# A fixed order for the first layernorm tiles, the third tile's statistics on ScalarE, and three x tiles loaded ahead of w_in

## The chip, the cores and the metric

One core of one Trainium2 chip. The metric is the device time of one execution in microseconds (us), lower is better. The engines are called as the profile calls them: PE (TensorE matmuls), PEld (TensorE weight loads), DVE (VectorE), ACT (ScalarE), POOL (GpSimd), and SPq for the queue that issues the DMAs. A ratio is the mean time of one kernel's fast runs over the mean of the other's fast runs of the same rounds, so it is not quite the ratio of the medians quoted beside it.

## The reference, cut to what matters

```python
x = A_x                                     # 1 x 2048 x 640, bf16
xn = _layernorm(x, axis=-1)                 # every path starts here
return x + A(xn, ...) + B(xn, ...)
# B: z = gelu(xn @ w_in); z1, z2 = halves of z; z2 = layernorm(z2)
#    g = w_sp @ z2 + b_sp ("spatial");  result (z1 * g) @ w_out
# A: a state-space scan: Bu = xn @ B_bar, h[t] = L*h[t-1] + Bu[t], y = 2*Re(h @ C)
```

The 2048 rows are 16 tiles of 128 rows, x0 to x15. Nothing but warm-up can run on PE before tile 0 is loaded, normalised and transposed.

## The kernel before

Each step of the program is an operation with declared reads, writes and an estimated duration. A small scheduler in the program walks the operations in estimated time and fixes, for each engine, **one order of instructions**. Estimated times decide that order and nothing else. On the chip, each engine keeps its order and waits at the head of its queue, as DVE does below for 1.24 us.

```python
FIRST = "x0 x1 h002 x2 h025 x3 h105 x4 x5"     # order of the first loads on SPq
# x2: tile 2 (160 KB).  h002, h025: w_in's second half, columns 0-431, k tiles 0-1 and 2-4
# (216 and 324 KB).  h105: columns 432-863, k tiles 0-4 (540 KB)
...
NW = 11                                         # warm-up matmuls, 128x512, on a zero tile
...
ACT_LN = (6, 8, 10, 12)                         # tiles whose statistics ACT computes

def ln_x(i):
    if i in ACT_LN:
        act(Copy,   accum_out=sum)              # lnsum: two passes on ACT
        act(Square, accum_out=sum of squares)   # lnsq
        dve(mean); dve(mean*mean); dve(variance)          # lnm, lnmm, lnv: 128x1 each
    else:
        dve(bn_stats, x[:, 0:320]); dve(bn_stats, x[:, 320:640]); dve(bn_aggr)   # statistics a, b, aggregate
    dve(variance + 1e-5)                        # lne
    pool((variance + eps) ** -0.5)              # rstd
    dve((x - mean) * rstd)                      # xn, 128x640
# ... cut ...
for i in range(5):
    ln_x(i)
xn_T(0, 0)          # T0: five PE transposes, then copies of PSUM by ACT (3/5) and DVE (2/5)
xn_T(1, 1)          # T1
z2_half(0, 0, 2)    # ten 128x432 matmuls on tiles 0 and 1, w_in columns 0-431
z2_half(1, 0, 3)
xn_T(2, 0)          # T2
z2_half(0, 1, 6)
xn_T(3, 1)          # T3
# ... cut: from tile 6 on, the transposes are DMAs; then "bu" (B matmuls), z1, spatial, output
```

## Time and profile before

| | before |
|---|---|
| median of the first 3 runs | 267.07 us (267.0 to 268.37) |
| span of the profiled execution | 265.7 us |
| PE busy | 259.6 us (98%) |
| PE idle at the two first transposes | 1.27 + 0.45 us |
| PE idle at 21 us, for a DMA transpose | 0.35 us |

The page's first part gives busy time, share of the span and instruction count of each engine.

```profile
PE 259.6 (98%) x1517; PEld 154.3 (58%) x1521; DVE 239.1 (90%) x574; ACT 174.1 (66%) x315; POOL 24.5 (9%) x41
```

PE is the engine to feed, and its gaps are few. The next lines are the timeline of PE in the kernel before: start, duration, engine, source line, operation, tiles, count, and in brackets how long the engine had been idle and what ended it.

```profile
1.31 4.75 PE L485 MATMUL ps<-arena 128*128 128x512 bf16 x11 [1.31 <-POOL arena L479]
7.33 0.45 PE L558 MATMUL ps<-arena 128*128 128x128 bf16 x5 [1.27 <-DVE arena L542]
8.23 0.45 PE L558 MATMUL ps<-arena 128*128 128x128 bf16 x5 [0.45 <-DVE arena L542]
8.53 2.03 PE L615 MATMUL ps<-arena 128*128 128x432 bf16 x10
10.39 0.44 PE L558 MATMUL ps<-arena 128*128 128x128 bf16 x5
...
21.36 18.42 PE L594 MATMUL ps<-arena 128*128 128x432 bf16 x100 [0.35 <-DMA arena<-arena]
39.84 20.45 PE L677 MATMUL ps<-arena 128*128 128x512 bf16 x93
```

The lines are the warm-ups, T0, T1, the first z2 matmuls, T2, the wait for the first DMA-transposed tile, and the first "bu" matmuls. The next view is the same kernel's DVE timeline around the gap.

```profile
4.92 0.21 DVE L533 BATCH_NORM_AGGREGATE arena<-arena 128x2 f32<-128x12 f32 x1
6.37 0.50 DVE L531 BATCH_NORM_STATS2 arena<-arena 128x6 f32<-128x320 bf16 x1 [1.24 <-DMA arena<-in_A_x_dram]
6.78 0.14 DVE L535 TENSOR_SCALAR arena<-arena 128x1 f32<-128x1 f32 x1
6.84 0.44 DVE L542 TENSOR_SCALAR arena<-arena 128x640 bf16<-128x640 bf16 x1
```

At 5.13 DVE has finished tile 1's statistics. The next instruction in its queue is tile **2's** first statistics, and x2 has not landed. Behind it stand tile 1's epsilon add (6.78) and tile 0's normalise (6.84). Both could have run. T0 follows at 7.33.

### The profile page before, as it was taken

The numbers are of one execution on the slowest core, as the hardware profiler recorded it, in microseconds if no ns is written. First come the engines' busy times: TensorE is split into PE (matmuls) and PEld (weight loads), VectorE is DVE, ScalarE is ACT, GpSimd is POOL, SyncE is SP. The second block draws the span as 40 slices with busy tenths as digits, with TensorE's granted clock in tenths as the row PEclk, the third lists the DMA queues.
The fourth block names the chain that finished last, engine by engine and source line by source line (L and its number), as shares of the span: only waits on it lengthen the run. The fifth ranks groups of instructions, "written<-read, shape, count | busy, mean of one in ns | idle before, by whom it ended". The sixth has DMA issues, their size and how long they took to land.

```text
span 265.7 us, 4351 instructions
## 1 busy us (share of the span) xinstructions
PE 259.6 (98%) x1517; PEld 154.3 (58%) x1521; DVE 239.1 (90%) x574; ACT 174.1 (66%) x315; POOL 24.5 (9%) x41
## 2 busy tenths in 40 slices
PE   7899999999999999999999999999999999999996
PEld 2454554444446777755555545555567777777774
DVE  3899999998999999999999999999999999976342
ACT  2699999989997545533233294584999999931110
POOL 3345176104000000000000000000000000000000
DMA  6957799996002755499979978969343566755411
GB/s 173 366 77 125 165 222 233 294 228 127 0 0 45 210 164 163 116 263 136 218 157 202 225 139 191 218 147 276 86 135 92 128 180 147 182 147 125 120 52 49
DMA packets 88243, 41.98 MB, mean 158 GB/s; under 512 B 70974, under 2 KB 88222, under 8 KB 88222
## 3 DMA queue, kind: packets, MB, share of 16 engines
q1 hardware_dynamic: 88078, 41.66, 66.2%
q8 instruction: 12, 0.20, 0.3%
q14 instruction: 9, 0.07, 0.1%
q10 hardware_dynamic: 144, 0.05, 0.1%
HBM read 12.27 MB, written 12.45 MB: 93 GB/s over the span
## 4 chain that ended last, share of the span: by engine, by line
PE 63%; DVE 21%; DMA 5%; ACT 5%; issue 3%; POOL 1%; SPq 0%; DVEq 0%
PE ps L594 18%; PE ps L677 16%; PE ps L1111 14%; PE ps L1123 11%; DVE arena L949 4%; PE ps L992 4%; ACT arena L784 4%; DVE arena L1012 3%; DVE arena L729 3%; DMA arena<-arena 2%; DMA arena<-in_A_x_dram 2%; DMA arena<-in_B_w_sp_dram 2%; DVE arena L914 1%; DVE arena L1033 1%; DVE arena L707 1%
## 5 line engine op out<-in xcount | busy, mean ns | idle before, releaser
L992 PE MATMUL ps<-arena 128*128 128x432 bf16 x448 | 82.4, 346 | 0.0
L992 PEld LDWEIGHTS ps<-arena 128*128 128x128 bf16 x448 | 43.6, 98 | 38.7 <-ACT arena L1005 1.5
L594 PE MATMUL ps<-arena 128*128 128x432 bf16 x280 | 51.8, 346 | 0.3 <-DMA arena<-arena 0.3
L784 ACT ACTIVATE arena<-arena 128x512 bf16<-128x512 bf16 x70 | 45.3, 717 | 2.2 <-DVE arena L749 2.1
L594 PEld LDWEIGHTS ps<-arena 128*128 128x128 bf16 x280 | 34.6, 124 | 16.7 <-DMA arena<-arena 0.8
L1111 PE MATMUL ps<-arena 128*128 128x320 bf16 x280 | 43.3, 299 | 0.2 <-ACT ps L1146 0.2
L677 PE MATMUL ps<-arena 128*128 128x512 bf16 x196 | 43.0, 379 | 0.2
L1005 ACT ACTIVATE arena<-ps,arena 128x432 f32<-128x432 f32 (+1 forms) x32 | 19.6, 617 | 30.3 <-PE ps L992 30.2
L1123 PE MATMUL ps<-arena 128*128 128x320 bf16 (+3 forms) x231 | 35.6, 295 | 0.0
L1111 PEld LDWEIGHTS ps<-arena 128*128 128x128 bf16 x280 | 27.2, 97 | 11.4 <-ACT ps L1146 0.5
L677 PEld LDWEIGHTS ps<-arena 128*128 128x128 bf16 x200 | 19.6, 98 | 23.5
L1138 DVE TENSOR_TENSOR arena<-ps,arena 128x320 bf16<-128x320 f32 (+1 forms) x40 | 18.9, 487 | 11.9 <-PE ps L1123 11.3
L1123 PEld LDWEIGHTS ps<-arena 128*128 128x128 bf16 (+1 forms) x231 | 22.3, 98 | 8.3
L707 DVE SCALAR_TENSOR_TENSOR arena<-arena 128x512 f32<-128x512 bf16 x35 | 25.8, 748 | 0.4 <-ACT arena L683 0.4
L788 DVE TENSOR_TENSOR arena<-arena 128x1024 bf16<-128x1024 bf16 (+1 forms) x42 | 23.9, 599 | 0.1
L683 ACT CAST arena<-ps 128x512 bf16<-128x512 f32 x40 | 21.3, 606 | 2.7 <-PE ps L677 2.7
L663 ACT ACTIVATE arena<-ps 128x864 bf16<-128x864 f32 x16 | 14.3, 891 | 13.5 <-PE ps L594 13.4
L949 DVE TENSOR_TENSOR arena<-arena 128x1024 bf16<-128x1024 bf16 x32 | 21.1, 688 | 0.9 <-DMA arena<-in_B_w_sp_dram 0.9
L729 DVE TENSOR_TENSOR arena<-arena 128x512 f32<-128x512 f32 (+2 forms) x40 | 21.3, 554 | 0.0
L1146 ACT COPY ps<-ps 128x320 f32<-128x320 f32 x16 | 6.7, 417 | 15.9 <-PE ps L1111 15.9
L709 DVE SCALAR_TENSOR_TENSOR arena<-arena 128x256 bf16<-128x256 bf16 (+1 forms) x35 | 16.7, 479 | 0.0
L712 DVE SCALAR_TENSOR_TENSOR arena<-arena 128x256 bf16<-128x256 bf16 (+1 forms) x35 | 16.6, 480 | 0.0
(103 smaller groups left out, 261.3 us busy)
## 6 DMA issues: line engine op xcount, KB each, us to landing
g_scratch<-arena SPq DMA_DIRECT2D x16, 224.0 KB, 3.5
z_scratch<-arena SPq DMA_DIRECT2D x16, 216.0 KB, 2.3
arena<-z_scratch SPq DMA_DIRECT2D x8, 432.0 KB, 5.3
arena<-in_A_x_dram SPq DMA_DIRECT2D x16, 160.0 KB, 3.8
base_scratch<-arena SPq DMA_DIRECT2D x16, 160.0 KB, 2.5
arena<-base_scratch SPq DMA_DIRECT2D x16, 160.0 KB, 2.3
out_dram<-arena SPq DMA_DIRECT2D x15, 160.0 KB, 2.3
arena<-in_B_w_in_dram SPq DMA_DIRECT2D x6, 216.0 KB, 4.2
```

Of the source, the lines that this page charges most:

```text
L594: r = e.matmul(ps[:, b + h, 0:FG], lhs(k), winv[:, k, hcol * FH + h * FG:hcol * FH + (h + 1) * FG], start=(k == 0), stop=(k == ND - 1))
L677: r = e.matmul(ps[:, b + ri, :], btv[:, ri, k, q * 128:(q + 1) * 128], xnTv[:, k, tq * 512:(tq + 1) * 512], start=(k == 0), stop=(k == ND ...
L683: act(lambda e, ri=ri: e.copy(o[:, ri, tq], ps[:, b + ri, :].rearrange("p (m j) -> p j m", j=8)), [bank(b + ri)], [l_m.iv((q * 8 + j) * 10 ...
L707: dve(lambda e: e.scalar_tensor_tensor(tv, prev, lr, cur, op0=ALU.mult, op1=ALU.add), pr + [l_iv(q, j)] + cr, [t.iv()], cd(512) + PTR, nm ...
L729: tt = lambda o, a, b, op: (lambda e: e.tensor_tensor(o, a, b, op))
L784: act(lambda e, pv=pv, hv=hv, lo=lo, sc=sc: e.activation(pv, hv[:, lo:lo + 2, 1:257], ACT.Identity, scale=sc), [h.iv(), Civ(cn)], [m.iv((q ...
L788: dve(lambda e, mv=mv, lq=lq: e.tensor_tensor(lq, lq, mv, ALU.add), li + [m.iv(0, 1024 * n)], li, cd(512 * n, 2), "fix%s%d%d" % (nm, q0, j))
L949: dve(lambda e: e.tensor_tensor(o.ap(1024), x.ap(1024), y.ap(1024), op), [x.iv(), y.iv()], [o.iv()], cd(1024, 2), "%s_%d" % (name, j))
L992: r = e.matmul(ps[:, bk, 0:FG], lv_[:, k, :], rv[k], start=(first and k == 0), stop=(k == 7), skip_group_check=True)
L1005: act(lambda e: e.activation(o, pb(bk), ACT.Identity, bias=bias), [bank(bk)] + bi, [dst], ca(FG, psum=True, ptr=1), name)
L1111: r = e.matmul(ps[:, bk, c0:c1], lf(q), rf(q)[:, c0:c1], start=(first and q == 0), stop=(q == 4), skip_group_check=True)
L1123: r = e.matmul(ps[:, bk, c0:c1], gv[0:kk, k, :], wov[0:kk, k, n * HD + c0:n * HD + c1], start=(first and k == 0), stop=(k == 6), skip_grou ...
```

## The change

The intent: let nothing that waits for x2 stand in front of tiles 0 and 1. x2 is loaded ahead of w_in, its statistics go to ACT (idle then), and added reads force DVE to finish tile 1 before it touches tiles 2 and 3.

```diff
-        FIRST = "x0 x1 h002 x2 h025 x3 h105 x4 x5"
+        FIRST = "x0 x1 x2 h002 h025 x3 h105 x4 x5"
-        ACT_LN = (6, 8, 10, 12)
+        ACT_LN = (2, 5, 8, 11)
                 dve(lambda e: e.tensor_scalar(mean, stv[:, i, 0:1], 1.0 / D, None, op0=ALU.mult),
-                    [siv(i, 0, 1)], [mi], 0.07, "lnm%d" % i)
+                    [siv(i, 0, 1)] + ([xns[1].iv()] if i == 2 else []), [mi], 0.07, "lnm%d" % i)
             else:
+                held = [xns[max(1, i - 2)].iv()] if 2 <= i < 4 else []
-                dve(lambda e: e.bn_stats(stv[:, i, 0:6], x[:, 0:320]), [xm.iv()], ...)
+                dve(lambda e: e.bn_stats(stv[:, i, 0:6], x[:, 0:320]), [xm.iv()] + held, ...)
# (the second bn_stats likewise)
```

A read that the instruction doesn't need is a way to tell the scheduler an order. The rest of the program is untouched, but the scheduler reorders much of DVE and ACT after the head, since its estimated times shift. PE's order stays the same.

More of the change, by code (lines that the diff above doesn't have):

```diff
@@ L530, in ln_x @@
             else:
-                dve(lambda e: e.bn_stats(stv[:, i, 0:6], x[:, 0:320]), [xm.iv()], [siv(i, 0, 6)], 0.41, "bn%da" % i)
-                dve(lambda e: e.bn_stats(stv[:, i, 6:12], x[:, 320:640]), [xm.iv()], [siv(i, 6, 12)], 0.41, "bn%db" % i)
+                held = [xns[max(1, i - 2)].iv()] if 2 <= i < 4 else []
+                dve(lambda e: e.bn_stats(stv[:, i, 0:6], x[:, 0:320]), [xm.iv()] + held, [siv(i, 0, 6)], 0.41, "bn%da" % i)
+                dve(lambda e: e.bn_stats(stv[:, i, 6:12], x[:, 320:640]), [xm.iv()] + held, [siv(i, 6, 12)], 0.41, "bn%db" % i)
                 dve(lambda e: e.bn_aggr(stv[:, i, 12:14], stv[:, i, 0:12]), [siv(i, 0, 12)], [siv(i, 12, 14)], 0.13,
```

## The prediction

> **What bounds it now.** The page gives PE busy 259.6 of 265.7 us (98%), DVE 90%, ACT 66%. The list of waits shows PE idle only at the head (1.31 us before its first instruction; 1.7 us at two transposes, L558 waiting for DVE's L542), 0.35 us at 21.0 for the first DMA-transposed x tile, and 0.16 us at 195.8 for an ACT copy. From 21.36 on PE has no other gap, so an earlier PE head moves the end, unless DVE or ACT, almost as full (stretches view: DVE 100% from 130 to 220, ACT 100% from 185 to 220), then make PE wait. Time: 267.07.
>
> **The head today.** VectorE is one in-order queue ("strict FIFO" in the Trainium skill, "PSUM — Partial Sum Buffer", section "Engine vs sequencer instructions"; the timeline agrees: at 5.13 DVE stops 1.24 us for x2's statistics, which land at about 6.35, though tile 1's epsilon add and tile 0's normalise stood ready behind them). So tile 0's normalise runs at 6.84 although its rstd was ready at 5.59, T0 at 7.33, the first z2 matmul at 8.53.
>
> **What the change does.**
> - Tile 2's statistics go to ACT (Copy 0.75+0.20 us, Square the same), idle then. DVE does xn0 at about 5.6, xn1 at 6.15. T0 moves from 7.33 to about 6.1, z2 of tile 0 from 8.53 to about 7.2. Gain here 1.3 us.
> - x2 swaps with the first w_in piece (issue about 0.4 us later, landing about 6.3 instead of 5.96: before it is needed). The bytes ahead of x3 are unchanged, so x3 still lands at about 7.7 (issue 3.12 + 4.6).
> - Most of the gain is lost there. In DVE's order, tile 2's mean-square, variance and epsilon steps stand behind tile 3's statistics, which now wait for x3. From 7.7: 0.41+0.41+0.4 to the epsilon add, POOL's power 0.55, so xn2 at about 9.55, as today (9.57). PE ends the first two z2 halves at about 9.2, waits about 0.8 us for T2, which starts at about 10.05 (10.39 now). PE gain left: about 0.3 us.
> - Tile 6 moves to DVE and its normalise from 16.1 to about 15.1, so its DMA transpose (4.8 us to landing) arrives before PE needs it: the 0.35 us wait goes.
> - VectorE's total work is unchanged (four ACT tiles before and after: 2,5,8,11 for 6,8,10,12), PE's and the bytes too.
> - The scheduler reshuffles the rest: z2_norm of tiles 8-15 earlier on ACT, the last scan slightly earlier on DVE. About neutral.
>
> **Critical share.** 0.3 + 0.35 = about 0.65 us of PE head. DVE gains little, so at 195.8, where PE already waits for ACT, part may be given back.
>
> **Prediction: 266.4 us**, 8 in 10 between 265.5 and 267.3. Faster by over 2%: 0.02; within 2%: 0.96; slower by over 2%: 0.02.
>
> **What would show it right or wrong.**
> - Timeline: T0 at about 6.1, first z2 matmul about 7.2; PE gap of 0.6-0.9 us before the third transpose, at about 9.2-10.
> - DVE idle before tile 3's first statistics, about 0.5-0.8 us, released by the x DMA.
> - The PE wait for the DMA-transposed tile (0.35) gone; first bu matmul (L677) at about 39.2, not 39.84.
> - The first out-projection product (L1111) about 0.6 us earlier, and PE waits of under 0.5 us in all after 40.
>
> **What would make it wrong.** x3 lands earlier (before 7), then the gain is up to 1.3 us. The B transpose (landing about 39.3 today, PE needs it at 39.84) does not move up with PE. The changed DVE order holds up h or s work, and PE waits at 112-200; then no gain.

## The result, and the profile after

| | before | after |
|---|---|---|
| median | 267.03 us (6 runs, 266.73 to 268.37) | 266.11 us (6 runs, 265.69 to 266.19) |
| ratio of the fast runs | | 0.9961, 95% interval 0.994 to 0.9981 |
| span of the profiled execution | 265.7 us | 263.9 us |
| first z2 matmul / first bu matmul | 8.53 / 39.84 us | 7.05 / 38.26 us |

The first part of the page, now of the changed kernel:

```profile
PE 258.7 (98%) x1517; PEld 154.4 (58%) x1521; DVE 238.8 (91%) x574; ACT 174.5 (66%) x315; POOL 24.0 (9%) x41
```

and its PE timeline (source lines have moved by two):

```profile
6.03 0.99 PE L560 MATMUL ps<-arena 128*128 128x128 bf16 x10 [0.58 <-DVE arena L544]
7.05 2.00 PE L617 MATMUL ps<-arena 128*128 128x432 bf16 x10
9.33 0.45 PE L560 MATMUL ps<-arena 128*128 128x128 bf16 x5 [0.28 <-DVE arena L544]
...
17.96 20.25 PE L596 MATMUL ps<-arena 128*128 128x432 bf16 x110
38.26 21.96 PE L679 MATMUL ps<-arena 128*128 128x512 bf16 x99
```

T0 starts 1.3 us earlier and the wait at 21 us is gone: the ten matmuls of each tile run on without a bracket. A wait of 0.28 us before T2 is new. The timeline of ACT in the changed kernel, at the line that takes x2, and then that of DVE, show why:

```profile
4.07 0.74 ACT L519 ACTIVATE arena<-arena 128x640 bf16<-128x640 bf16 x1 [1.83 <-DMA arena<-in_A_x_dram]
```

DVE:

```profile
5.52 0.98 DVE L544 TENSOR_SCALAR arena<-arena 128x640 bf16<-128x640 bf16 x2 [0.31 <-POOL arena L539]
6.95 0.49 DVE L533 BATCH_NORM_STATS2 arena<-arena 128x6 f32<-128x320 bf16 x1
7.36 0.14 DVE L525 TENSOR_TENSOR arena<-arena 128x1 f32<-128x1 f32 x1
8.00 0.15 DVE L537 TENSOR_SCALAR arena<-arena 128x1 f32<-128x1 f32 x1
8.82 0.97 DVE L544 TENSOR_SCALAR arena<-arena 128x640 bf16<-128x640 bf16 x2 [0.36 <-POOL arena L539]
```

ACT takes x2 at 4.07. Tiles 0 and 1 are normalised from 5.52, back to back. But tile 2's small steps (L525 at 7.36, its epsilon add L537 at 8.00) stand behind tile **3's** statistics at 6.95, which start when x3 lands, at 6.9. So tile 2 is normalised only from 8.82.

The trace pair says 1.8 us and the medians 0.9. The profiled executions took 267.48 us (before) and 265.69 us (after): the first is slower than its kernel's median, the second the fastest of its kernel. One pair of traces is one draw from each kernel, and the experiments had to begin with that.

### The profile page after: what moved, and what is told of

Read it like the earlier page. It is cut to its first block, busy times and chain, and to the rows that moved or that the text cites. A ratio compares the mean times of both kernels' runs of the same rounds, so it can differ in the third digit from the quotient of the medians.

```text
span 263.9 us, 4352 instructions
## 1 busy us (share of the span) xinstructions
PE 258.7 (98%) x1517; PEld 154.4 (58%) x1521; DVE 238.8 (91%) x574; ACT 174.5 (66%) x315; POOL 24.0 (9%) x41
## 4 chain that ended last, share of the span: by engine, by line
PE 95%; DMA 1%; SPq 1%; DVE 1%; issue 0%; POOL 0%
PE ps L994 31%; PE ps L596 19%; PE ps L679 16%; PE ps L1113 14%; PE ps L1125 12%; PE ps L617 2%; DMA arena<-in_A_x_dram 1%; SPq L370 1%; PE ps L560 0%; POOL arena L539 0%; DVE arena L544 0%; DVE arena L534 0%; DVE arena L1187 0%; DVE arena L537 0%; DVE arena L525 0%
## 5 line engine op out<-in xcount | busy, mean ns | idle before, releaser
L994 PEld LDWEIGHTS ps<-arena 128*128 128x128 bf16 x448 | 43.7, 98 | 38.3 <-ACT arena L1007 0.8
L1113 PE MATMUL ps<-arena 128*128 128x320 bf16 x280 | 43.1, 299 | 0.0
L665 ACT ACTIVATE arena<-ps 128x864 bf16<-128x864 f32 x16 | 14.3, 891 | 13.5 <-PE ps L596 13.4
```

The lines of the kernel that those rows point to most:

```text
L994: r = e.matmul(ps[:, bk, 0:FG], lv_[:, k, :], rv[k], start=(first and k == 0), stop=(k == 7), skip_group_check=True)
L1113: r = e.matmul(ps[:, bk, c0:c1], lf(q), rf(q)[:, c0:c1], start=(first and q == 0), stop=(q == 4), skip_group_check=True)
```

## The experiments

Theory A: the gain lies in the head, because a load that comes late no longer stands in front of ready work on DVE. Rival B: the load order is incidental, and the gain comes from the fixed order, the ACT tile or the reshuffled later order. Each call of four kernels ran on one chip, with its own runs of the kernel before beside them. The three calls were on three chips.

### e1, e2: both kernels again

No edit. What was expected of the changed kernel:

> The changed kernel unaltered, to see how far traces and times repeat. First record: 266.11 us, ratio 0.9961, but its trace spans 263.9 us against 265.7 of the kernel before, a difference of 1.8 us where the medians differ by 0.9. Theory A (head: x2 no longer blocks VectorE): ratio 0.994 to 0.998; first bu matmul (L679) at 38.0 to 39.2 us (39.84 before), x3's statistics start at 6.9 to 7.7 us, first z2 matmul at 7.05. If the trace's extra 0.9 us was luck of one execution, these come out later than 38.26 and 6.95.

and of the kernel before:

> The kernel before unaltered, a control for noise and a second trace of it: ratio 0.998 to 1.002; first z2 matmul 8.3 to 8.6 us, VectorE idle 0.9 to 1.3 us for x2, PE wait of 0.2 to 0.5 us for the first DMA-transposed tile, first bu matmul 39.5 to 39.9 us.

| | median, range (us) | ratio, interval | x2 / x3 landed | first z2 / first bu matmul |
|---|---|---|---|---|
| kernel before (11 runs) | 266.96, 265.65 to 268.5 | | | |
| e1 | 266.1, 265.61 to 266.46 | 0.996, 0.9929 to 0.9991 | 4.9 / 7.3 | 7.39 / 38.47 |
| e2 | 266.86, 266.19 to 269.16 | 1.001, 0.9964 to 1.0056 | 5.1 / 7.4 | 7.29 / 38.58 |

(Landings are issue time plus time to landing in the DMA view, so good to about 0.1 us.) The changed kernel repeats. The kernel before does not: in this trace x2 landed at 5.1 and not 6.3, DVE never waited for it, and the head was as early as the changed kernel's. The DVE and PE timelines of e2, at tile 2's first statistics and at the first z2 matmul:

```profile
5.10 0.49 DVE L531 BATCH_NORM_STATS2 arena<-arena 128x6 f32<-128x320 bf16 x1
7.29 2.00 PE L615 MATMUL ps<-arena 128*128 128x432 bf16 x10
```

The expectation for e2 (z2 at 8.3 to 8.6, bu at 39.5 to 39.9) missed by a microsecond. The late head of the first trace is something that happens in *some* executions.

So the distributions count. Over all calls, the kernel before ran 45 times (39 as reference, 6 as e2). 32 of the times lie between 265.65 and 267.85 (mean 266.77), 13 between 268.14 and 269.16 (mean 268.53). The gap of 0.29 us between them is hardly wider than others in the list (0.27), but the mean granted clock for each execution tells the groups apart: 10 of the 12 upper ones that have it show 0.994 and two 1.000, and none of the 27 lower ones that have it is below 0.999. (An estimate from these: 0.006 missing over 268 us is about 3.2 us at half clock.) The changed kernel's 12 runs all lie between 265.61 and 266.46 (mean 266.06), with clocks of 0.999 or more; its fastest run and that of the kernel before (265.65) are only 0.04 us apart. About 0.7 us of the gain is against the lower group; the rest of the 1.2 us between the means comes from the upper group being absent. The upper group is not equally common everywhere: 1 of 6 runs in the first record, then 4 of 17, 1 of 11 and 7 of 11 in the three calls. The changed kernel itself ran only beside the first two (5 of 23), so its 12 clean runs alone are weak evidence. With the variants below in which T0 does not wait for x2 (e3, e4, e5, e7, e8, e10, e12) there are 54 runs, and none is above 267.5.

### e3, e4: each half of the change alone

e3 is the kernel before with `FIRST = "x0 x1 x2 h002 h025 x3 h105 x4 x5"`: two loads swap, and all engines keep the order of the kernel before. e4 is the changed kernel with the old `FIRST`, so it has the changed kernel's orders with x2 behind w_in's first piece.

> The kernel before with x2's load ahead of w_in's first piece and nothing else: every compute engine's order is that of the kernel before, only two DMA issues swap. Theory A1 (the late x2 in front of tile 0's normalise was the whole loss; the DMA order alone cures it): x2 lands at about 4.1, xn0 at about 5.6, T0 at about 6.1, first z2 matmul 7.1 to 7.3 us, first bu matmul 38.2 to 38.9 us, ratio 0.994 to 0.997, no worse than the changed kernel. Rival B (the fixed order and ACT's tile 2 are what gains, or the later reshuffle is needed for the gain to reach the end): ratio 0.998 to 1.000, and either the head is not earlier or the PE waits grow at about 195 us.

> The changed kernel with the old load order (x2 behind w_in's first piece): compute orders are those of the changed kernel. Theory A1: x2 lands at 6.0 to 6.4, ACT (in order) does tile 2's two passes until about 8.2 before the copy of xnT0, so T0 starts at about 6.1 but the first z2 matmul only at 8.6 to 8.9, no gain in the head; ratio 0.998 to 1.001. Rival B (the fixed order and the ACT tile are the gain): first z2 matmul at 7.0 to 7.3, ratio 0.994 to 0.997.

Measured: e3 266.49 us (265.67 to 267.15), ratio 0.9971 (0.9934 to 1.0007); e4 266.39 us (265.99 to 266.75), ratio 0.9973 (0.9942 to 1.0004). PE's timeline of e3:

```profile
6.01 0.45 PE L558 MATMUL ps<-arena 128*128 128x128 bf16 x5 [0.42 <-DVE arena L542]
...
20.50 18.43 PE L594 MATMUL ps<-arena 128*128 128x432 bf16 x100 [0.56 <-DMA arena<-arena]
```

The load order alone cures the start (T0 at 6.01), but PE then waits 0.56 us for the first DMA-transposed tile, which the changed ACT tiles remove: in the changed kernel tile 6 is on DVE and is normalised earlier. (In e2, with the old ACT tiles and as early a head, this wait shows only in the weight loads, 0.55 us.) In e4, T0 starts early and its copy does not. ACT's timeline of e4:

```profile
5.75 0.74 ACT L519 ACTIVATE arena<-arena 128x640 bf16<-128x640 bf16 x1 [3.51 <-DMA arena<-in_A_x_dram]
6.61 0.74 ACT L521 ACTIVATE arena<-arena 128x640 bf16<-128x640 bf16 x1
7.35 0.46 ACT L564 COPY arena<-ps 128x384 bf16<-128x384 bf16 x1
```

The copy of transposed tile 0 (L564) stands behind ACT's two passes over x2, and the first z2 matmul starts at 7.86 after a wait of 1.01 us for it. I expected 8.6 to 8.9 and no gain; x2 landed at 5.7 and the ratio is 0.9973, so the loss was overstated. Both halves have medians better than the reference's and worse than the whole's 266.1, but both intervals reach just past 1. Neither A nor B is right alone: each half leaves a wait of its own in its trace. That the two halves need each other is not shown, because the intervals of e1, e3 and e4 overlap.

### e5, e11: x2 late on purpose

e5: `FIRST = "x0 x1 h002 h025 x2 x3 h105 x4 x5"` in the kernel before.

> The kernel before with x2's load moved back, behind both of w_in's first pieces; all compute orders as before. Theory A (in the kernel before the landing of x2 sets the head, because its statistics stand in front of tile 0's normalise on VectorE): x2 lands at 6.7 to 7.4 us, T0 starts at 7.6 to 8.5, first bu matmul at 40.0 to 41.0, ratio 1.002 to 1.006. Rival (x2 has slack; the gain lies in the later order): head and time unchanged, ratio 0.998 to 1.001.

Measured: 266.72 us (266.18 to 267.5), ratio 0.9988 (0.9964 to 1.0012), x2 landed at 7.3, T0 at 6.02. The expectation was wrong in its premise: the orders did **not** stay. The scheduler knew of the later load and by itself put tiles 0 and 1 ahead of tile 2's statistics. An x2 one microsecond later than in the first trace cost nothing against the kernel before: in this order T0 did not wait for it.

e11 is e5's load order with the order of every engine forced to be that of the kernel before.

> The kernel before with x2's load behind both first pieces of w_in and, unlike the earlier run of that name, the orders on every engine forced to be those of the kernel before (only two DMA issues swap). Theory A: x2 lands at 6.7 to 7.3 us, T0 at 7.5 to 8.2, first bu matmul at 40.0 to 41.5, median 267.4 to 268.8, ratio 1.002 to 1.008, and (theory C) executions of 268 to 270 us are common. Rival (x2 is not what sets the head): ratio 0.999 to 1.001.

Measured: 268.79 us (267.05 to 270.42) beside 268.28 for the reference, ratio 1.0044 (0.9997 to 1.009). x2 landed at 7.0, T0 started at 8.00. So with the same first loads T0 starts at 6.02 in one order and at 8.00 in the other: the order in front of a late load is what matters for T0. In time the two ratios, each against the kernel before in its own call, are about 1.5 us apart, but they come from two chips, and e11's interval reaches just below 1. The traced execution of e11 (270.42) was its slowest. First bu matmul: 43.1 us, later than the 40.0 to 41.5 expected. PE's timeline of e11 shows a second loss:

```profile
8.00 0.72 PE L620 MATMUL ps<-arena 128*128 128x128 bf16 x5 [2.81 <-DVE arena L604]
8.90 0.72 PE L620 MATMUL ps<-arena 128*128 128x128 bf16 x5 [0.18 <-DVE arena L604]
9.40 3.81 PE L677 MATMUL ps<-arena 128*128 128x432 bf16 x10
```

Ten 128x432 matmuls took 3.81 us, not 2.0. The view of stretches (PE busy, then the granted clock, DMA share, GB/s) of the same execution:

```profile
6.00:8.00 2.00, 0.00 (x1) 0.86 1.04 350
8.00:10.00 2.00, 1.82 (x12) 0.50 1.08 367
10.00:12.00 2.00, 2.00 (x7) 0.50 1.05 369
12.00:14.00 2.00, 2.00 (x11) 0.50 0.93 303
14.00:16.00 2.00, 2.00 (x15) 0.93 0.03 5
```

While PE stood idle for 2.81 us, its clock was halved. From the means (0.86 and 0.93 of two stretches of 2 us) the half clock lasted 0.56 + 6.0 + 0.28 = 6.8 us. The four runs of e11 above 268 us are the four whose mean clock is 0.994 or less.

### e6, e7: the head and the later order apart

In the first trace PE's weight loads wait for ACT late in the kernel, while PE counts as 100% busy. The weight-load timeline of the kernel before:

```profile
155.95 2.67 PEld L992 LDWEIGHTS ps<-arena 128*128 128x128 bf16 x16 [0.42 <-ACT arena L1005]
159.03 17.27 PEld L992 LDWEIGHTS ps<-arena 128*128 128x128 bf16 x96 [0.41 <-ACT arena L1005]
176.50 10.01 PEld L992 LDWEIGHTS ps<-arena 128*128 128x128 bf16 x56 [0.21 <-ACT arena L1005]
186.95 7.05 PEld L992 LDWEIGHTS ps<-arena 128*128 128x128 bf16 x40 [0.43 <-ACT arena L1005]
```

and of the changed kernel, all there is in that stage:

```profile
164.53 2.67 PEld L994 LDWEIGHTS ps<-arena 128*128 128x128 bf16 x16 [0.36 <-ACT arena L1007]
167.61 24.57 PEld L994 LDWEIGHTS ps<-arena 128*128 128x128 bf16 x136 [0.41 <-ACT arena L1007]
```

From the first spatial to the first output matmul, the old order took 82.27, 82.53 and 82.15 us (before, e2, e3), the new one 82.03, 82.00 and 81.92 (after, e1, e4). The Trainium skill, "Perfetto Trace Analysis", section "Tensor Engine Instruction (MATMUL, LD_WEIGHTS)", says that the profiler estimates the end of a PE instruction and does not observe it, so PE busy need not show such a wait. This trace agrees: from 150 to 170 us the PE row shows 20.00 busy of 20.00, across two weight-load waits of 0.4 us.

To see whether the later order causes it, e6 has the head of the kernel before and then the changed kernel's order on every engine; e7 has the changed kernel's head and then the old order. Edit, in outline:

```diff
+    def schedule_as(self, given): ...    # replay a given order per engine
         g.schedule()
+        g.schedule_as(GIVEN)             # e6: old order up to the last layernorm operation, then new
```

> The kernel before with its load order and its order up to the end of the layernorm statistics on every engine, but after that the order of the changed kernel. Theory A plus a second, smaller source seen in the traces (in the spatial stage PE's weight loads wait 1.3 to 1.8 us for ACT's evictions in the old order, 0.7 in the new): stage from the first spatial matmul (L992) to the first output matmul (L1111) 81.9 to 82.1 us, against 82.15 to 82.53 in the old order; head as in the kernel before; ratio 0.9975 to 1.000. If the later order is worth nothing, the stage stays at 82.2 to 82.5.

> The changed kernel (loads, ACT tiles, fixed order) but with the kernel before's order on every engine after the layernorm statistics. Theory A: first z2 matmul 7.0 to 7.4, first bu matmul 38.0 to 38.7, spatial stage 82.1 to 82.6 with weight-load waits of 1.3 to 1.8 us; ratio 0.995 to 0.998. If the later order carries the gain: ratio 0.999 or more in spite of the earlier head.

Reference of that call (11 runs): 266.86 us. e6: 266.72 us (266.26 to 268.17), ratio 0.9982 (0.9956 to 1.0007), stage 81.83 us. e7: 266.28 us (266.11 to 267.03), ratio 0.9974 (0.9951 to 0.9997), stage 81.80 us. The changed head with the old later order is enough for a gain: e7's interval stays below 1. What the later order adds is not settled by the times, because the two ratios differ by 0.0008 and their intervals reach about 0.0025 to either side. The other half of the expectation failed. e7 has the old later order, and its stage is among the shortest of all 14 traces (81.76 to 82.53). So the later order as such does not make the stage long; how far PE runs ahead of DVE and ACT may. That stays open.

It matters for what the head is worth. In all 14 traces the time from the first bu to the first spatial matmul is 72.15 to 72.38 us, and from the first output matmul to the end 71.38 to 71.44 us. So two traces differ only by when bu starts and by this stage. In the first pair nearly all of the difference is in the start of bu (1.58 us; the stage 0.24). Between e2 and e1, each near its kernel's usual time, bu starts only 0.11 us apart and the stages differ by 0.53. How the 0.7 us against the lower group divides between the head and this stage is therefore not shown.

e6's profiled execution was its slowest (268.17), so it is a trace from the upper group, with the old loads and the old head. Its PE timeline:

```profile
6.97 0.71 PE L620 MATMUL ps<-arena 128*128 128x128 bf16 x5 [0.79 <-DVE arena L604]
...
8.38 3.12 PE L677 MATMUL ps<-arena 128*128 128x432 bf16 x10
```

Again half speed: each z2 matmul's weight load starts 0.36 us after the one before (8.74, 9.10, 9.46, 9.82, 10.18) in place of 0.18 later on, until about 10.5. The clock view does not show it: it reads 1.00 from 0 to 16 us, also over the first warm-ups, which start 0.43 us apart. In this trace half speed is read from the spacing alone. DVE waited 0.98 us for x2 here, PE 0.79 us for T0.

### e8: tile 2's small steps ahead of x3

If x3 is what limits the changed kernel, take tile 2's steps out from behind it:

```diff
-                held = [xns[max(1, i - 2)].iv()] if 2 <= i < 4 else []
+                held = [xns[1].iv(), siv(2, 14, 15)] if i == 3 else []   # after tile 2's epsilon add
```

> The changed kernel with tile 3's statistics held until tile 2's epsilon add has run, so that tile 2's small steps no longer stand behind a load (x3); eight places change in VectorE's order, none on ACT or the DMA queue. Theory A, with x3 as what limits the changed kernel: PE's wait before the third transpose (0.28 and 0.36 us in two traces) goes, third transpose at 8.9 to 9.4 instead of 9.33 and 9.75, first bu matmul about 0.3 us earlier than the changed kernel at the same x2 landing (37.9 to 38.3); ratio 0.993 to 0.9965. Rival (x3 has slack or PE would wait elsewhere): the wait stays, or a wait of the same size comes up at the fourth transpose or at w_in.

Measured: 266.0 us (265.58 to 266.14), ratio 0.9956 (0.9935 to 0.9978), which cannot be told from the changed kernel's 0.996. The PE timeline of e8, and after it the PEld timeline's first line for the matmuls that follow T2:

```profile
9.13 0.44 PE L560 MATMUL ps<-arena 128*128 128x128 bf16 x5
9.68 1.09 PE L617 MATMUL ps<-arena 128*128 128x432 bf16 x5
10.99 0.45 PE L560 MATMUL ps<-arena 128*128 128x128 bf16 x5 [0.23 <-DVE arena L544]
```

PEld:

```profile
9.67 0.66 PEld L617 LDWEIGHTS ps<-arena 128*128 128x128 bf16 x5 [0.28 <-DMA arena<-in_B_w_in_dram]
```

The wait at T2 is gone, as theory A has it, and the rival was right about the rest: two waits of about the same size take its place. The weights of the next matmuls (h105) landed at 9.6. And T3 waits, because the scheduler put tile 4's statistics in front of tile 3's normalise and DVE stood 0.83 us for x4: the same trap, two tiles on. The first bu matmul came at 38.74, later than the 37.9 to 38.3 expected.

### e9, e10: warm-up matmuls alone

Theory C: the upper group comes from PE's idle time after the warm-ups. The Trainium skill, "TensorE: Matmul & The Clock Gate", section "What's actually happening", says that PE starts at half clock and gets the full clock after a busy window of about 3.4 us, on windows that run freely and don't start with the kernel. The traces here agree: the warm-ups start 0.43 us apart at first and 0.22 us apart from about 4.1 us on in e11 and 6.3 us in e9, and in e11 the full clock comes at about 4.1, is lost at 7.4 and is back at 14.3, that is after one and two such windows. e9: the kernel before with `NW = 13`, all other engines' orders forced to stay. e10: the changed kernel with `NW = 8`, orders unchanged.

> The kernel before with 13 instead of 11 warm-up matmuls (0.43 us each), its orders on all other engines forced to be those of the kernel before, so that PE has less idle time between the warm-ups and T0. Theory C (part of the loss, and the slow executions of 268 to 269 us, come from PE's idle gap of 0.8 to 1.3 us after the warm-ups: the full clock is then granted [...]at 9.7 to 11.5 us in place of 4.8 to 7.0, and z2 matmuls take 0.36 instead of 0.18 us until then): no execution above 267.6, median 266.4 to 266.9, ratio 0.996 to 0.999, although x2 and VectorE's order are untouched. Theory A alone: T0 still waits for x2; ratio 0.999 to 1.001 and executions above 268 still come up.

> The changed kernel with 8 instead of 11 warm-up matmuls, all other orders unchanged: the warm-ups end at about 4.8 us, 1.2 us before T0 can start, a gap as long as the one in the kernel before. Theory C: the full clock comes late in most executions (8 to 11.5 us), the first z2 matmuls take 0.36 us each, the times spread to 267 to 268.5 and the median rises to 266.6 to 267.8, ratio 0.998 to 1.003. Theory A alone: T0, the z2 start and the time stay as in the changed kernel, ratio 0.995 to 0.997, spread under 1 us.

| | median, range (us) | ratio, interval |
|---|---|---|
| kernel before (11 runs) | 268.28, 266.32 to 268.81 (7 above 268) | |
| e9, before with 13 warm-ups | 266.77, 266.58 to 267.67 (0 of 6 above 268) | 0.9972, 0.9936 to 1.0008 |
| e10, after with 8 warm-ups | 266.27, 265.54 to 266.88 (0 of 6 above 268) | 0.9949, 0.9908 to 0.9989 |

In this call 7 of the 11 runs of the kernel before are above 268, and none of the 18 of e9, e10 and e12: more warm-ups and an early head each go with the absence of the upper group. e9 fits: with x2's load and DVE's order untouched, the upper group is gone, and all six clocks are 1.000. Its one trace does not test a late x2, which landed there by 5.1 (the slowest run, 267.67, is just over my bound of 267.6; it is the traced one, and x3 landed at 8.6 in it). e10 does not: a gap of 1.06 us between the warm-ups and T0 did not delay the clock in its trace (ten z2 matmuls in 2.0 us), the median stayed, and the spread grew only to 1.3 us. So a gap of this length is not enough by itself. The old head's sparse stretch is longer (warm-ups end at 6.1, z2 starts at 8.4 to 8.5), and e10's warm-ups end earlier; which of the two matters is open.

### e12: without the fixed order

```diff
-                    [siv(i, 0, 1)] + ([xns[1].iv()] if i == 2 else []), [mi], 0.07, "lnm%d" % i)
+                    [siv(i, 0, 1)], [mi], 0.07, "lnm%d" % i)
-                held = [xns[max(1, i - 2)].iv()] if 2 <= i < 4 else []
+                held = []
```

> The changed kernel without the added reads that fix VectorE's order: loads and ACT tiles as changed, the scheduler free to order. It puts tile 2's mean and mean-square steps ahead of tile 0's normalise, its variance ahead of tile 1's. If the fixed order is needed: tile 0's and 1's normalise wait for ACT's two passes over x2, T0 at 6.2 to 6.9, first z2 matmul 7.3 to 8.0, ratio 0.996 to 0.999. If not (x2 lands at 4.1 to 5.1, ACT is done in time, and x3 no longer stands in front of tile 2): T0 at about 6.0 to 6.2, third transpose without PE wait at 8.9 to 9.3, ratio 0.994 to 0.9965.

Measured: 265.85 us (265.61 to 267.09), ratio 0.9941 (0.9904 to 0.9978) in the call with the slow reference. PE's timeline:

```profile
9.09 0.44 PE L560 MATMUL ps<-arena 128*128 128x128 bf16 x5
...
38.63 6.64 PE L679 MATMUL ps<-arena 128*128 128x512 bf16 x30 [0.67 <-DMA arena<-in_A_B_im_dram]
```

T2 does not wait, and what PE gained it gives back at 38 us, where B's transposed load is not there yet. The added reads are not needed for the median: with x2 loaded early and on ACT, the scheduler's own order is as good. Its range is wider (one run at 267.09), and six runs can't tell whether the fixed order guards against that. A PE wait for B also shows in e2, e5, e7 and e9 (0.2 to 0.7 us): it may cap what an earlier head can bring.

## Why the prediction was right or wrong

- *Time.* Predicted 266.4 (265.5 to 267.3), measured 266.11. Within 2%, as forecast. That the number fits is in part luck: of the 1.2 us between the means, 0.5 comes from the absent upper group, which the prediction did not have.
- *The head: T0 at about 6.1, first z2 matmul about 7.2.* Right: 6.03 and 7.05 (6.11 and 7.39 in e1).
- *"Most of the gain is lost there": x3 at 7.7, T2 at about 10.05 after a PE wait of 0.8 us, 0.3 us left.* The mechanism was right: tile 2's steps do stand behind tile 3's statistics, and e8 removed the wait by moving them. The size was off. x3 landed at 6.9 and 7.3 in the two traces of the changed kernel, T2 started at 9.33 and 9.75 after waits of 0.28 and 0.36 us. The DVE idle time of 0.5 to 0.8 us before tile 3's statistics was under 0.1 and 0.17 us. I took one trace's landing for a constant, though I had named an x3 before 7 as what would make me wrong. With the same DVE order in the head, e10 (x3 at 7.5) and e7 (x3 at 7.8) show waits of 0.97 and 1.13 us, so the term really ranges that far.
- *The 0.35 us wait for the DMA transpose goes.* Right. With the old ACT tiles and an early head, PE waits 0.56 us there in e3, and in e2 the weight loads 0.55.
- *First bu matmul at about 39.2, first output product 0.6 us earlier.* 38.26 (38.47 in e1), and 1.8 us earlier (192.44 against 194.26) in the trace pair. The pair overstates: the profiled execution of the kernel before was slower than its median.
- *PE waits under 0.5 us in all after 40.* Right by the PE row, which has none; the weight loads wait for ACT 0.8 us in the spatial stage and 0.2 us at the output products.
- *The premise "the head today".* It described one execution. In another (e2) x2 landed in time and there was no such gap. Not foreseen at all: the 45 runs of the kernel before form two groups 1.8 us apart in their means, and the changed kernel has only shown the lower one. Half-speed z2 matmuls are shown in the two traces that fell into slow executions (e6, e11), and more warm-up matmuls removed the upper group in six runs (e9). For the slow executions of the kernel before itself there is only the mean clock, 0.994 in 10 of 12; that all of them have this cause is inferred.

## What to carry to other kernels

On an in-order engine, ask of each instruction near the start whether it waits for a load, and what ready work stands behind it; a scheduler that works from estimated landing times will put the trap back one tile later. Before explaining a difference below 1%, profile the old kernel twice and look at all its times: the gain here is in good part a narrower distribution (0.5 of 1.2 us). When PE is warmed up ahead of its first data, idle time between the warm-ups and the real work can cost twice, once as the gap and once as half clock after it: it did in e11 (2.81 us idle, then 6.8 us at half clock, which began in the gap), and did not in e10 (1.06 us).

## What the Trainium skill lacked or had wrong

- "TensorE: Matmul & The Clock Gate", section "What's actually happening": its table gives the half clock "after ≥1 idle window (~3.4µs)". In e11 an idle gap of 2.81 us after full clock was enough, and the half clock lasted 6.8 us, about two of the page's windows. The page has no measure of how busy a window must be: 1.06 us without matmuls did not hold the full clock back (e10), while in e6 a 0.79 us gap and sparse transposes went with half speed until about 10.5 us.
- "PSUM — Partial Sum Buffer", section "Engine vs sequencer instructions": its "strict FIFO" for DVE and ACT holds here (1.24 us at 5.13 in the kernel before, the copy behind ACT's two passes in e4). It does not say that such waits can make the head vary from run to run, as it did here with the landing of x2 (first z2 matmul at 8.53 and 7.29 in two traces of one kernel).
- "DMA: Bandwidth & Descriptors" has no figure for how much the landing of one load varies between executions. Here a 160 KB load of unchanged issue time and place in the queue (x2 of the kernel before) landed 4.2 us after issue in one trace and 3.0 in another, and x3, issued at 3.1, landed between 6.9 and 8.6.
